# Hidden features of SwiGLU side by side, three tiles to an operation; first stage and last product rearranged

## The chip, the cores and the metric

The kernel runs on one core of one Trainium2 chip. The metric is the device time of one execution in microseconds (us). Engines are called as in the profile: PE is the matrix engine (PEld its weight loads), DVE the vector engine, ACT the activation engine, POOL the general one, SP the engine that does little but issue transfers. Each engine works through its own queue in order. On ACT and SP that queue also holds the transfers they issue, and a transfer whose data is not ready holds up what stands behind it.

## The reference

A gated recurrence with an outer product as state (4 batches, 8 heads, 768 tokens, head size 48), followed by a SwiGLU block on 3072 tokens of width 384 with 1536 inner features:

```python
f = 1.0 / (1.0 + np.exp(-f_logit))
for t in range(S):
    state = f[:, :, t, :, None] * state + np.einsum('bhd,bhe->bhde', k[:, :, t], v[:, :, t])
    y[:, :, t] = np.einsum('bhd,bhde->bhe', q[:, :, t], state)
x = y.transpose(0, 2, 1, 3).reshape(B * S, H * D)
g = x @ w_gate
out = (g * (1.0 / (1.0 + np.exp(-g))) * (x @ w_val)) @ w_out
```

The three weight arrays arrive in double precision and are turned into single precision on the chip. All else is float32.

## The kernel before

`short_path` does the work. A token chunk has 128 tokens of each of the four batches; there are six chunks, 0 to 5. The recurrence of one batch in one chunk is a *unit*; units 0 to 3 belong to chunk 0, units 4 to 7 to chunk 1, and so on. `attention(u)` (L518) is a generator that gives out one unit in 13 steps: gates (a sigmoid on ACT; for chunks 0 and 1 after PE has transposed f, for the later ones on f as it was loaded), a backward scan `tail` (L549), kT, a forward scan `head` (L562), qT, the scores `sc` (L586), their masking into A (L596), the product y, and the new state. `load` (L413) issues a unit's f, k, q and v transfers on SP.

**First stage** (up to L1157). Units 0 to 3 run one behind another (`run`). Between their steps the first weight pieces of 768 KB are fetched (`fetches`, SP), prepared by two ACT operations (`sizes`, L459 and L461) and put together by four or five DVE operations (`joins`, L467 to L473). The scratch of `sizes` has two buffers, so a `sizes` waits for the join two before it. The first four pairs of sizes and joins are half pieces: gate and val tile 0, gate and val tile 1. Then `mlp_plain(0)` begins: gate and val products of chunk 0 (L712) with Silu on ACT (L724) and a product on DVE (L728), together with the first steps of unit 4. `in_order` (L684) fixes the order of PE, DVE and ACT as written for this stage; SP's order is left to the planner.

**Second stage.** The rest of `mlp_plain(0)` takes turns with units 4 to 7. Here the planner decides the order of all engines. The down product of chunk 0 is `downs_abreast`.

**Third stage** (L1186 to L1219), chunks 1 to 5. The hidden products of a chunk are `mlp_fifteen` (L839). A product of 3x3 by 3x2 blocks is done with 15 instead of 18 block products. The token side has sums of token blocks, made by `token_sums` (L847) on DVE. One `triple(j)` covers the fifteen products (L887, four matmuls each: gate and val, two parts) of one of four sets of features. ACT copies a product's bank aside (L892), DVE adds and subtracts (L786, L789), and `finish` makes Silu (ACT, L903) and the product with val (DVE, L837). The triples come in the order 0, 2, 1, 3, so that hidden tiles with even numbers are complete after two of them. The down product is `down_seven` (L967), seven block products instead of eight. It needs sums of hidden blocks: `hidden_sums(j)` (two DVE operations per tile, for six tiles), then the first block of each tile is rewritten after `one` and the third after `two`. The seven are `one, six, two, three, four, five, seven`, each in two parts of 12 matmuls (L990; L1054 in `seven`), and `put_out` (L997) issues the result transfers.

A unit's steps, the token sums and the down weight sums enter by due times (`come_in`, L1191); the token sums of the next chunk are due two units of time before the chunk ends, thus ahead of the second part of `seven`. What is given to `lag` is written out one piece later, behind the next piece's matmuls. `in_order` fixes PE, DVE and ACT, not SP.

PSUM banks of this stage: tag A two, B one, o two (tag c shares them). A hidden tile is 128 partitions x 4 blocks x 256 tokens, six per chunk, a tag of six buffers (L702). `seven` writes both its halves into one bank of tag A. Its sums (`ob`) go out on ACT's queue, the last one of the kernel on SP's.

Of the kernel before, what the change touches and what calls it, by code (L numbers as in the profile page):

```python
# [9 lines left out]
FP32 = mybir.dt.float32  # L10
I32 = mybir.dt.int32
U32 = mybir.dt.uint32
AF = mybir.ActivationFunctionType
# [276 lines left out]
def short_path(ctx, tc, ident, least, judge, q, k, v, f_logit, moe_w_gate, moe_w_val, moe_w_out, out):  # L290
# [9 lines left out]
    nc = tc.nc  # L300
    B, H, S, D = q.shape
    C = 128
# [59 lines left out]
    def pairs(t, off=0):  # L362
        return t[:, off:off + HP * N1].rearrange("p (a t) -> p a t", t=N1)
# [151 lines left out]
    def bank(name):  # L515
        return banks[-1].tile([128, 512], FP32, tag="a", name=name)

    def attention(u):  # L518
        b, c = units[u]
        fr, kr, qr = (raw[nm][u % NRAW] for nm in "fkq")  # L520
# [10 lines left out]
        if c >= SQUARES:  # L531
            nc.scalar.activation(squares("f"), squares("f"), AF.Sigmoid)
        else:
            p = transposed("fTp", fr)
            nc.scalar.activation(pairs(gate)[:, :, 1:N1], p, AF.Sigmoid)
        yield
        if c >= SQUARES:
            nc.vector.transpose(in_turn(pairs(gate)[:, :, 1:N1]), squares("f"))
# [160 lines left out]
    TH = TB // 2  # L699
    FH = DFF // 2  # L700

    def hidden_tile():  # L702

        return ffn.tile([128, 4, TH], FP32, tag="h", name="h", bufs=NP)

    def mlp_plain(c):
        h = {}

        def product(w, j, name):
            p = fps.tile([128, 512], FP32, tag="m", name=name)[:, 0:TB]  # L710
            for i in range(KT):
                nc.tensor.matmul(p, lhsT=w[:, j, i, :], rhs=xT[c][:, i, :],  # L712
                                 start=(i == 0), stop=(i == KT - 1))
            return p

        def part(j):
            if j % NP not in h:
                h[j % NP] = hidden_tile()
            k = 2 * (j // NP)
            return h[j % NP][:, k:k + 2, :].rearrange("p a t -> p (a t)")  # L720

        def gate(j):
            p = product(w_gate, j, "gate")
            nc.scalar.activation(part(j), p, AF.Silu)  # L724

        def val(j):
            p = product(w_val, j, "val")
            nc.vector.tensor_tensor(part(j), part(j), p, ALU.mult)  # L728

        return ([lambda j=j, f=f: f(j) for f, j in ((gate, 0), (val, 0), (gate, 1), (val, 1))] +  # L730
                [lambda j=j, f=f: f(j) for i in range(2, NF, 2) for f in (gate, val) for j in (i, i + 1)],
                downs_abreast(c, h))

    def down_part(p, c, h, b, n):

        j = n // 2 + n % 2 * NP
        nc.tensor.matmul(p, lhsT=h[n // 2][:, n % 2 * 2 + b // 2, b % 2 * C:(b % 2 + 1) * C], rhs=w_out[:, j, :],  # L737
                         start=(n == 0), stop=(n == NF - 1))

    def out_rooms():  # L740
# [44 lines left out]
    def plus(dst, a, b):  # L785
        nc.vector.tensor_tensor(dst, a, b, ALU.add)  # L786
# [49 lines left out]
    def lag(f, *args):  # L836
        lagging.append(lambda: f(*args))  # L837

    def mlp_fifteen(c):  # L839
# [6 lines left out]

        def token_sums():  # L847
            x = comb.tile([128, 9, TH], FP32, tag="xs", name="xs")
            for n, nm in enumerate(("t14", "t15", "t8", "t9", "t2", "t1", "t4", "t11", "t5")):
                tokens[nm] = x[:, n, :]  # L850
            t = tokens
            minus(t["t14"], b21, b31)
            minus_both(t["t15"], b31, b32)
            plus(t["t8"], b21, t["t15"])
            plus(t["t9"], b12, b22)
            minus_both(t["t2"], t["t9"], t["t14"])
            plus(t["t1"], b12, b32)
            minus(t["t5"], b32, b11)
            plus(t["t4"], b11, t["t9"])
            minus_both(t["t11"], t["t4"], b21)  # L860
            plus(b12, b11, b12)
            plus(b31, b11, b31)
# [4 lines left out]

        def out_part(i, n, j):
            f = i * NJ + j
            if f % NP not in h:  # L870
                h[f % NP] = hidden_tile()
            return h[f % NP][:, 2 * (f // NP) + n, :]

        def triple(j):
            p, got = {}, {}
# [80 lines left out]
        order = list(range(0, NJ, 2)) + list(range(1, NJ, 2))  # L956
        pieces = [f for j in order for f in triple(j)]
        half = len(PRODUCTS) * (NJ // 2)
        ready = [sorted({(i * NJ + j) % NP for i in range(KT) for j in range(n, NJ, 2)}) for n in range(2)]
        for i, n in enumerate(ready[0]):  # L960
            pieces.insert(half + 10 + 3 * i, (0, lambda n=n: lag(hidden_sums, n)))
        pieces.append((0, finish_late))
        pieces.append(last[0])
        pieces += [(0, lambda n=n: lag(hidden_sums, n)) for n in ready[1]]
        return token_sums, pieces + last[1:]

    def down_seven(c, h):  # L967
# [1 line left out]


        DH = DM // 2
        s1 = [comb.tile([128, TH], FP32, tag=f"hs{j}", name=f"hs{j}") for j in range(NP)]
        b11, b12 = w_out[:, 0:NP, 0:DH], w_out[:, 0:NP, DH:DM]
        b21, b22 = w_out[:, NP:NF, 0:DH], w_out[:, NP:NF, DH:DM]
        kept = {}
        order = [*range(0, NP, 2), *range(1, NP, 2)]

        def hidden_sums(j):
            a11, a21, a12, a22 = (h[j][:, k, :] for k in range(4))
            plus(s1[j], a21, a22)  # L980
            minus(a21, a11, a21)

        def bank2(name, tag):
            pool = {"A": banks_a, "B": banks_b, "o": banks_o}[tag]
            return pool.tile([128, 512], FP32, tag=tag, name=name)[:, 0:DM].rearrange("p (n d) -> p n d", n=2)

        def add(p, lhsTs, rhs, first, part):
            for j in order[part * NP // 2:(part + 1) * NP // 2]:
                for n in range(2):
                    nc.tensor.matmul(p[:, n, :], lhsT=lhsTs[j][:, n * C:(n + 1) * C], rhs=rhs[:, j, :],  # L990
                                     start=first and j == order[0] and n == 0, stop=j == order[-1],
                                     skip_group_check=True)

        def of_h(k):
            return [h[j][:, k, :] for j in range(NP)]

        def put_out(half, n, queue):  # L997
            t0 = (2 * half + n) * S + c * C
# [2 lines left out]
        def one(part):  # L1001
            if part == 0:
                kept["o", 0], kept["o", 1] = out_rooms()
                kept["u"], kept["u5"] = (comb.tile([128, 2, TH], FP32, tag=t, name=t)[:, :, 0:DH]
                                         for t in ("c12", "c22"))
                kept["p"] = bank2("o11", "B")
            add(kept["p"], of_h(0), b11, True, part)
            if part:
                nc.scalar.copy(kept["u"], kept["p"])
                for j in order:  # L1010
                    lag(minus, h[j][:, 0, :], s1[j], h[j][:, 0, :])

        def two(part):
            add(kept["p"], of_h(2), b21, False, part)
            if part:
                nc.scalar.copy(kept["o", 0][:, :, 0:DH], kept["p"])
                for j in order:
                    lag(minus, h[j][:, 2, :], h[j][:, 2, :], h[j][:, 0, :])

        def three(part):  # L1020
            if part == 0:
# [5 lines left out]
        def four(part):  # L1027
            if part == 0:
                kept["p5"] = bank2("o5", "B")
            add(kept["p5"], s1, down_sums[1], True, part)  # L1030
            if part:
                lag(plus, kept["u5"], kept["u"], kept["p5"])

# [14 lines left out]
            add(kept["p4"], of_h(3), down_sums[4], True, part)  # L1048

        def seven(n):  # L1050
            if n == 0:
                kept["p"] = bank2("o3", "A")
            for j in order:
                nc.tensor.matmul(kept["p"][:, n, :], lhsT=h[j][:, 2, n * C:(n + 1) * C], rhs=b22[:, j, :],  # L1054
                                 start=n == 0 and j == order[0], stop=j == order[-1], skip_group_check=True)
            lag(plus, kept["o", 0][:, n, DH:DM], kept["u5"][:, n, :], kept["p"][:, n, :])
            lag(put_out, 0, n, nc.sync if n and c == NCH - 1 else nc.scalar)

        return hidden_sums, [(DOWN / 2, lambda f=f, part=part: f(part))
                             for f in (one, six, two, three, four, five, seven) for part in range(2)]  # L1060
# [45 lines left out]
    def run(b, *steps):  # L1106
        for s in steps:
            assert done[b] == s
            done[b] += 1
            for _ in range((3, 1, 4, 2, 3)[s]):  # L1110
                next(first[b])

    def load_ahead(u):

        if u + NRAW < B:
            load(u + NRAW, "fkq")
        load(u + 1, "v")
        fetches.pop(0)()
        if u + NRAW >= B:
            load(u + NRAW, "fkq")  # L1120

    run(0, 0, 1, 2)
# [1 line left out]
    for b in range(1, B):  # L1124
        if b == 1:
            run(1, 0)
            keep_warm(6)
        run(b, 1)
        run(b - 1, 3)
        run(b, 2)  # L1130
        load_ahead(b)
        if b + 1 < B:
            run(b + 1, 0)
        else:
            sizes.pop(0)()
        run(b - 1, 4)
    run(B - 1, 3)
    joins.pop(0)()
    run(B - 1, 4)

    hidden, last = mlp_plain(0)
    steps = attention_steps(1)
    for _ in range(2):
        sizes.pop(0)()
        joins.pop(0)()
    load(B + 1, "v")
    for _ in range(2):
        sizes.pop(0)()
    hidden[0]()
# [2 lines left out]
    joins.pop(0)()  # L1152
    hidden[1]()
    weights()
    hidden[2]()
    steps.pop(0)()
    in_order(mark, (mybir.EngineType.PE, mybir.EngineType.DVE, mybir.EngineType.Activation))  # L1157

# [135 lines left out]
```

## Time and profile before

| | us |
|---|---|
| median of 3 runs | 622.11 (620.12 to 622.82) |
| the profiled execution | 620.31 |
| its span | 618.6 |
| PE busy | 599.7 |
| DVE busy | 500.3 |
| ACT busy | 293.5 |
| first 52 us: PE busy / DVE busy | 43.75 / 44.00 |
| 147 to 210 us (fifteen products of chunk 1): PE / DVE | 62.54 / 60.73 |
| 244 to 307 us (the same of chunk 2): PE / DVE | 62.14 / 51.68 |

The profile comes from one execution. A line of a timeline reads: start, duration, engine, line of the kernel, operation, output and input, shape, and in brackets the idle time before it and what ended it. `x4` means four instructions drawn together. Matmuls overlap, so the duration of one line reaches into the next; the distance between starts is what one costs. A line of the waits reads: who waited, for whom, us in total, times, longest. PE's granted clock was full until the work ended (1.00 in every window to 584 us).

### The profile page before, as it was taken

Reading aid. Unit: us, or ns where it says so; the run is one execution under the profiler, and the core shown is the slowest. Engines: PE = TensorE matmul, PEld = TensorE weight load, DVE = VectorE, ACT = ScalarE, POOL = GpSimd, SP = SyncE. Lnnn points to the kernel's source line nnn. Section 1 sums busy time; section 2 is a strip of 40 time slices with the busy share of each in tenths; the row PEclk is TensorE's granted clock in tenths of the full one; section 3 lists DMA queues with packets and bytes.
Section 4 is the critical chain, followed back from the end, with each engine's and each line's share of the span. In section 5 each row is a group of like instructions: output and inputs, shape, how many; then the busy total and the mean of one; then the engine's idle time right before and its main releaser. Section 6 shows DMA issues by size and latency. Waiting matters only on the chain.

```text
span 618.6 us, 10913 instructions
## 1 busy us (share of the span) xinstructions
PE 599.7 (97%) x4060; PEld 490.1 (79%) x4060; DVE 500.3 (81%) x961; ACT 293.5 (47%) x535; POOL 5.0 (1%) x27
## 2 busy tenths in 40 slices
PE   7898999999999999999999999999999999999995
PEld 4744545667888898888899788899888889888895
DVE  7889999878999978868897877987887985566741
ACT  2485645313875621557711557632367640366600
POOL 1000000000000000000000000000000000000000
PEclk9999999999999999999999999999999999999998
DMA  9999583005231324222224320323321300100001
GB/s 150 236 246 254 172 231 92 5 23 161 63 86 51 85 61 125 69 48 64 51 77 117 91 52 19 84 62 95 107 75 33 81 6 10 52 2 0 1 2 56
DMA packets 95678, 50.95 MB, mean 82 GB/s; under 512 B 56064, under 2 KB 89472, under 8 KB 95616
## 3 DMA queue, kind: packets, MB, share of 16 engines
q1 hardware_dynamic: 92304, 45.64, 30.5%
q10 hardware_dynamic: 3312, 4.52, 2.0%
q8 instruction: 34, 0.56, 0.4%
q14 instruction: 28, 0.23, 0.1%
HBM read 42.47 MB, written 4.72 MB: 76 GB/s over the span
## 4 chain that ended last, share of the span: by engine, by line
PE 77%; DVE 12%; ACT 4%; DMA 3%; issue 2%; SPq 1%; ACTq 0%; DVEq 0%
PE o L990 16%; PE A L887 15%; PE B L887 11%; PE o L737 5%; PE o L887 5%; PE c L887 5%; PE sc L586 4%; PE val L712 4%; PE gate L712 3%; PE y L618 2%; PE kt L590 2%; PE y L614 1%; PE dS L659 1%; DVE head L562 1%; DMA fraw<-in_f_logit_dram 1%
## 5 line engine op out<-in xcount | busy, mean ns | idle before, releaser
L887 PE MATMUL A<-xs,w_both 128*128 128x256 f32 x240 | 62.6, 383 | 3.5 <-ACT c L892 2.3
L990 PE MATMUL o<-w_out,h 128*128 128x192 f32 x360 | 62.1, 328 | 0.2 <-ACT aside L892 0.2
L990 PEld LDWEIGHTS o<-w_out,h 128*128 128x128 f32 x360 | 58.6, 190 | 0.8 <-ACT aside L892 0.4
L887 PEld LDWEIGHTS A<-xs,w_both 128*128 128x128 f32 x240 | 44.5, 190 | 12.4 <-ACT c L892 3.9
L892 ACT COPY c<-A 128x512 f32<-128x512 f32 x40 | 23.3, 583 | 65.1 <-DVE ob L786 33.9
L786 DVE TENSOR_TENSOR c<-c,aside 128x512 f32<-128x512 f32 x60 | 41.1, 686 | 14.8 <-ACT aside L892 13.8
L892 ACT COPY aside<-A 128x512 f32<-128x512 f32 x60 | 35.0, 583 | 33.0 <-PE A L887 33.0
L789 DVE TENSOR_TENSOR c<-c,aside 128x512 f32<-128x512 f32 x60 | 41.2, 687 | 7.3 <-ACT aside L892 7.3
L837 DVE TENSOR_TENSOR h<-h,c 128x256 f32<-128x256 f32 x100 | 41.2, 421 | 7.0 <-ACT h L903 6.7
L990 PE MATMUL o<-ws,h 128*128 128x192 f32 x240 | 41.7, 328 | 0.0
L887 PE MATMUL B<-xT,extra 128*128 128x256 f32 x160 | 41.4, 382 | 0.0
L887 PE MATMUL c<-xT,w_both 128*128 128x256 f32 x160 | 41.3, 381 | 0.0
L887 PE MATMUL A<-xs,extra 128*128 128x256 f32 x160 | 41.2, 380 | 0.0
L887 PE MATMUL B<-xs,w_both 128*128 128x256 f32 x160 | 41.1, 380 | 0.0
L903 ACT ACTIVATE h<-c 128x256 f32<-128x256 f32 x100 | 39.2, 415 | 3.0 <-DVE c L789 1.9
L892 ACT COPY aside<-B 128x512 f32<-128x512 f32 x60 | 34.9, 582 | 10.6 <-PE B L887 10.2
L990 PEld LDWEIGHTS o<-ws,h 128*128 128x128 f32 x240 | 39.2, 190 | 0.3 <-issue 0.2
L789 DVE TENSOR_TENSOR c<-o,c 128x512 f32<-128x512 f32 x40 | 27.5, 689 | 14.6 <-ACT h L903 9.5
L596 DVE TENSOR_TENSOR A<-sc,causal 128x512 f32<-128x512 f32 x48 | 30.6, 678 | 6.0 <-PE sc L586 6.0
L887 PEld LDWEIGHTS B<-xs,w_both 128*128 128x128 f32 x160 | 30.4, 190 | 4.1
L887 PEld LDWEIGHTS c<-xT,w_both 128*128 128x128 f32 x160 | 30.2, 190 | 4.3 <-DVE c L789 0.2
L887 PEld LDWEIGHTS A<-xs,extra 128*128 128x128 f32 x160 | 30.3, 190 | 4.1
(134 smaller groups left out, 1155.0 us busy)
## 6 DMA issues: line engine op xcount, KB each, us to landing
fsquares<-in_f_logit_dram SPq DMA_DIRECT2D x64, 96.0 KB, 2.3
ksquares<-in_k_dram SPq DMA_DIRECT2D x64, 96.0 KB, 2.3
qsquares<-in_q_dram SPq DMA_DIRECT2D x64, 96.0 KB, 2.3
v<-in_v_dram SPq DMA_DIRECT2D x24, 192.0 KB, 3.3
w<-in_moe_w_gate_dram SPq DMA_DIRECT2D x6, 768.0 KB, 6.1
w<-in_moe_w_val_dram SPq DMA_DIRECT2D x6, 768.0 KB, 5.6
w<-in_moe_w_out_dram SPq DMA_DIRECT2D x6, 768.0 KB, 5.3
out_dram<-ob ACTq DMA_DIRECT2D x23, 192.0 KB, 2.0
```

The lines of the kernel that those rows point to most:

```text
L586: nc.tensor.matmul(sc[par][:, a * C:(a + 1) * C], lhsT=kT[r, a, :], rhs=qT[r, a, :], start=True, stop=True)
L590: nc.tensor.transpose(p[:, a * C:(a + 1) * C], kT[:, a, :], ident)
L596: nc.vector.tensor_tensor(A[:, par], sc[par].rearrange("p (a t) -> p a t", t=C), causal.unsqueeze(1).broadcast_to((128, HP, C)), ALU.mult)
L712: nc.tensor.matmul(p, lhsT=w[:, j, i, :], rhs=xT[c][:, i, :], start=(i == 0), stop=(i == KT - 1))
L737: nc.tensor.matmul(p, lhsT=h[n // 2][:, n % 2 * 2 + b // 2, b % 2 * C:(b % 2 + 1) * C], rhs=w_out[:, j, :], start=(n == 0), stop=(n == NF ...
L786: nc.vector.tensor_tensor(dst, a, b, ALU.add)
L789: nc.vector.tensor_tensor(dst, a, b, ALU.subtract)
L837: lagging.append(lambda: f(*args))
L887: nc.tensor.matmul(p[name][:, n, :], lhsT=weights_of[a][:, n, j, :], rhs=tokens[b], start=fresh and n == 0, stop=True, skip_group_check=True)
L892: nc.scalar.copy(t, p[name])
L903: nc.scalar.activation(dst, src[:, 0, :], AF.Silu)
L990: nc.tensor.matmul(p[:, n, :], lhsT=lhsTs[j][:, n * C:(n + 1) * C], rhs=rhs[:, j, :], start=first and j == order[0] and n == 0, stop=j == ...
```

## The change

1. **Hidden tiles.** Two tiles of 128 x 3 x 4 x 256 instead of six of 128 x 4 x 256: one holds features 0, 2, 4, the other 1, 3, 5. `hidden_sums` and the two rewritings handle three features in one operation. The even sums are all due after the twelfth product of the third triple, where they were due after products 10, 12 and 14.
2. **Token sums.** t9 and t1, which stand beside each other now, are made in one operation of 2 x 256.
3. **seven.** Each half has a bank of its own, the first of tag A, the second of tag o; all its result transfers go out on SP.
4. **First stage.** Unit 4's sigmoid is taken on f as loaded, before the first Silu; behind the transposition stands a Copy. The first three sizes and joins move up by a step. Unit 5's f, k and q are loaded together with its v, later. SP's order is fixed as written too.

```diff
+    ahead = set()
+    def sigmoid_ahead(u):
+        fr = raw["f"][u % NRAW]
+        nc.scalar.activation(fr, fr, AF.Sigmoid)
+        ahead.add(u)
@@ attention
-            nc.scalar.activation(pairs(gate)[:, :, 1:N1], p, AF.Sigmoid)
+            nc.scalar.activation(pairs(gate)[:, :, 1:N1], p, AF.Copy if u in ahead else AF.Sigmoid)
@@ hidden tiles
-    def hidden_tile():
-        return ffn.tile([128, 4, TH], FP32, tag="h", name="h", bufs=NP)
+    def hidden_tile(h, j):
+        if j % 2 not in h:
+            h[j % 2] = ffn.tile([128, NP // 2, 4, TH], FP32, tag="h", name="h", bufs=2)
+        return h[j % 2][:, j // 2]
@@ token_sums
-            for n, nm in enumerate(("t14", "t15", "t8", "t9", "t2", "t1", "t4", "t11", "t5")):
+            for n, nm in enumerate(("t14", "t15", "t8", "t9", "t1", "t2", "t4", "t11", "t5")):
...
-            plus(t["t9"], b12, b22)
+            two = (128, 2, TH)
+            plus(x[:, 3:5], b12.unsqueeze(1).broadcast_to(two), xT[c][:, 1:3, TH:2 * TH])
             minus_both(t["t2"], t["t9"], t["t14"])
-            plus(t["t1"], b12, b32)
@@ mlp_fifteen, order of the pieces
-        for i, n in enumerate(ready[0]):
-            pieces.insert(half + 10 + 3 * i, (0, lambda n=n: lag(hidden_sums, n)))
-        pieces.append((0, finish_late))
-        pieces.append(last[0])
-        pieces += [(0, lambda n=n: lag(hidden_sums, n)) for n in ready[1]]
+        pieces.insert(half + 12, (0, lambda: lag(hidden_sums, 0)))
+        pieces += [(0, finish_late), last[0], (0, lambda: lag(hidden_sums, 1))]
@@ down_seven
-        def hidden_sums(j):
-            a11, a21, a12, a22 = (h[j][:, k, :] for k in range(4))
-            plus(s1[j], a21, a22)
+        def hidden_sums(odd):
+            a11, a21, a12, a22 = (h[odd][:, :, k, :] for k in range(4))
+            plus(s1[odd], a21, a22)
             minus(a21, a11, a21)
...
-                for j in order:
-                    lag(minus, h[j][:, 0, :], s1[j], h[j][:, 0, :])
+                for odd in range(2):
+                    lag(minus, h[odd][:, :, 0, :], s1[odd], h[odd][:, :, 0, :])
...
-                for j in order:
-                    lag(minus, h[j][:, 2, :], h[j][:, 2, :], h[j][:, 0, :])
+                for odd in range(2):
+                    lag(minus, h[odd][:, :, 2, :], h[odd][:, :, 2, :], h[odd][:, :, 0, :])
...
         def seven(n):
-            if n == 0:
-                kept["p"] = bank2("o3", "A")
+            p = bank2("o3", "Ao"[n])[:, n, :]
             for j in order:
...
-            lag(put_out, 0, n, nc.sync if n and c == NCH - 1 else nc.scalar)
+            lag(put_out, 0, n, nc.sync)
@@ first stage
-        if u + NRAW >= B:
+        if u + NRAW == B:
             load(u + NRAW, "fkq")
...
+    joins.pop(0)()
+    sizes.pop(0)()
     run(B - 1, 3)
+    sizes.pop(0)()
     joins.pop(0)()
     run(B - 1, 4)
...
-    for _ in range(2):
-        sizes.pop(0)()
-        joins.pop(0)()
-    load(B + 1, "v")
+    sigmoid_ahead(B)
+    joins.pop(0)()
     for _ in range(2):
         sizes.pop(0)()
     hidden[0]()
...
     weights()
+    load(B + 1)
     hidden[2]()
     steps.pop(0)()
-    in_order(mark, (mybir.EngineType.PE, mybir.EngineType.DVE, mybir.EngineType.Activation))
+    in_order(mark, (mybir.EngineType.PE, mybir.EngineType.DVE, mybir.EngineType.Activation, mybir.EngineType.SP))
```

## The prediction

> **What bounds the kernel now.** First the page's busy line: PE is busy 599.7 of 618.6 us. So the time is PE's work plus PE's gaps, and what another engine gives up counts only where it ends a gap.
>
> ```profile
> span 618.6 us, 10913 instructions
> PE 599.7 (97%) x4060; PEld 490.1 (79%) x4060; DVE 500.3 (81%) x961; ACT 293.5 (47%) x535; POOL 5.0 (1%) x27
> ```
>
> Second, the waits of PE: who ended a gap, total us, times, longest.
>
> ```profile
> PE sc L586 <- DVE qT L568: 3.3, 3, 1.8
> PE A L887 <- ACT c L892: 2.3, 4, 0.6
> PE A L887 <- ACT aside L892: 1.3, 5, 0.3
> ```
>
> DVE, 81% busy, ends no gap after the first 52 us. ACT, 47% busy, ends nine of them. Third, the timeline of ACT and of PE at the beginning of a block of fifteen products (chunk 1 ends, chunk 2 begins; the other three look alike).
>
> ```profile
> 241.66 4.71 ACTq L999 DMA_DIRECT2D out_dram<-ob  x3
> 246.41 0.58 ACT L892 COPY c<-A 128x512 f32<-128x512 f32 x1 [8.62 <-DVE ob L786]
> ```
>
> ```profile
> 245.45 1.03 PE L887 MATMUL o<-xT,w_both 128*128 128x256 f32 x4
> 247.05 1.13 PE L887 MATMUL A<-xs,w_both 128*128 128x256 f32 x4 [0.57 <-ACT c L892]
> 248.02 1.03 PE L887 MATMUL B<-xT,extra 128*128 128x256 f32 x4
> ```
>
> ACT holds the result transfers of the last quarter of the output. They wait for DVE's last sums (ob), which DVE makes after the token sums, at 245.6 to 246.2. Behind them in ACT's queue stands the copy of product 0, which was ready near 244.8. PE's product 3 needs a bank of tag A and stalls. Last, the end of the first stage and of the kernel.
>
> ```profile
> 39.28 1.28 ACT L535 ACT_TABLE_LOAD   x1
> 42.78 0.56 DVE L467 TENSOR_SCALAR top<-top 128x768 f32<-128x768 f32 x1 [1.59 <-ACT top L461]
> 46.38 1.22 DVE L549 TENSOR_TENSOR_SCAN tails<-gates,ones 128x516 f32<-128x516 f32 x1
> 51.67 1.16 PE L586 MATMUL sc<-qT,kT 48*128 48x128 f32 x16 [1.81 <-DVE qT L568]
> ```
>
> ```profile
> 611.98 0.62 DVE L786 TENSOR_TENSOR ob<-c,o 128x192 f32<-128x192 f32 x2 [2.29 <-PE o L1054]
> 612.66 0.38 SPq L999 DMA_DIRECT2D out_dram<-ob  x1
> ```
>
> **Result transfers from ACT to SP (seven).** Two issues of some 0.35 us leave ACT per chunk, and so does their wait. The copy of product 0 then starts at 244.8 and ends at 245.4; product 3 is due at 245.45 + 0.865 (the spacing of products) = 246.31. If it takes the bank of the first last product instead, that is free when DVE has read it, near 245.9: also in time. What a stall costs is read from product 4: due at 247.18, it began at 248.02, so 0.84 (0.57 of gap, the rest refilling). Four boundaries: 3.4 us. Against this speaks the Trainium skill, "DMA: Bandwidth & Descriptors", section "Issuing engines are not separate DMA queues": all issuing engines feed the same 16 DMA engines, and another issuer saves only the issue time, usually small. By that rule ACT gains 0.7 us a chunk and PE nothing. The row decides otherwise: what ACT loses is not the issue but 8.62 us of waiting in front of a copy, which the rule doesn't speak of. I take 3.4; by the rule it is 0, and that end goes into the range. On SP the two wait until 246.2; the next transfers behind them are the f loads at 252.23, which the transposed gates release at 251. Nothing is held up.
>
> **Separate banks for the last product.** The second half takes a bank of tag o. Its two slots held six's and five's sums, which DVE has read by 241.63 and 240.5; PE wants one at 241.77. Cost 0, at most 0.3 a chunk (one short gap), 1.5 in all. Inside a chunk DVE makes the token sums first, so the early read pays only at the very end: there the first half's sum need no longer wait for 611.98 but starts at 610.0, the second's at 611.98 instead of 612.25, and its transfer is issued 0.3 earlier. That transfer took 3.9 us to land while its neighbour flew beside it; a pair at 609.7 took 2.6 and 2.8, pairs at the chunk boundaries 1.9. Alone I take 2.8: 0.3 + 1.1 = 1.4, between 0.3 and 2.3.
>
> **The beginning.** Unit 4's sigmoid moves in front of the Silus and its later activation is a Copy: the table loads at 39.28 and 42.76 go (1.28 each), one activation of 128x512 (0.60) comes. Two size pairs (1.1 each) and a join (1.9) move up by one step. DVE idles 1.25 before the masking of unit 3 at 27.86: the first join fills it and pushes the masking to 28.5, and that unit's last copy, which the first gate product needs, ends near 31.0. The first gate product now starts at 31.14 waiting for that join: no change. Followed forward on ACT and DVE in their order (a size pair may start when the join two before it has ended): joins end at 31.6, 33.4, 35.3 and 38.3; Silu's remaining load at 35.2, Silu to 37.0, the Copy to 37.6, sizes of the fourth weight piece (landed at 36.3) to 39.3, its join to 42.4. Behind that join DVE has unit 4's scan: 42.4 instead of 46.38. From scan to sc is 5.3 us, so sc is ready at 47.7, before PE asks at 49.9: the 1.81 go. The Trainium skill, "ScalarE: Activation LUTs", section "What ACT_TABLE_LOAD costs", puts a switch at 2.66 us, a 1.38 drain included. The trace has 1.29 from the load at 37.37 to its Silu at 38.66, so no drain is paid here. By the page the remaining load would put the scan at 43.8 and sc at 49.1: still in time, so the sum is the same by both. Between 39 and 50 PE's order is the planner's, not written out; if it keeps sc too early the gain is nothing. I take 1.8, ends 0 and 2.
>
> SP's order is now fixed here. Its sequence of bytes is nearly the present one: unit 3's f lands behind the same weight piece (19.3). Unit 5's f, k, q move behind the fifth piece and land near 44 instead of 38 to 41; PE uses f at 59.27, a cover of 15 us. Unit 6's k and q wait on SP for unit 4's transposes (39.4 to 40.4) and hold up the sixth piece, fetched at 40.64 today: under 1 us, PE needs it at 62. Without these covers each would cost what it is late.
>
> **Three tiles side by side.** Per chunk 24 operations of 128x256 become 8 of 128x768. Six in a row take 2.10, so one costs 0.34. A strided 128x1152 took 1.35 and 128x512 takes 0.69, 1.03 ns an element; so 768 take 0.95, or 0.86 in a row.
>
> ```profile
> 201.27 1.35 DVE L789 TENSOR_TENSOR ws<-w_out,ws 128x1152 f32<-128x1152 f32 x1
> 219.54 2.10 DVE L789 TENSOR_TENSOR h<-hs,h 128x256 f32<-128x256 f32 x6
> ```
>
> 24 x 0.335 = 8.0 against 8 x 0.86 = 6.9; the joined token sum saves another 0.08. DVE gains 1.2 a chunk, 6 in all, and on the path 0: no gap of PE in these stages names DVE. The even sums now come as one block of 1.7 at the twelfth product instead of 0.7 thrice; what follows it on DVE (sums that free asides) is up to 1.05 later, once a chunk. ACT's asides wait for that, and PE for ACT. I take 0, since three asides and two A banks lie between; all of it passed on would be 5.3. The two h tiles become free with the last product of a chunk; their first new write is the Silu at product 9, 10 us later.
>
> **Sum.** 618.6 - 3.4 - 1.4 - 1.8 = 612.0 span. The profiled run took 620.31 (1.7 around the span) and lies 1.8 below the median of the runs shown, 622.11. So 613.7 in such a run, 615.5 against the median.
>
> **Rivals.**
> 1. The transfers help, the rest doesn't (planner keeps sc early, the last transfer lands in 3.9): 622.1 - 3.4 - 0.3 = 618.4. For it: PE's order there is unknown. Against: DVE's chain has 4 us taken out.
> 2. The blocks of merged sums reach PE: + 5.3 on 615.5, 620.8. For it: from 147 to 210 DVE is busy 60.7 of 63, and ACT waits there for DVE's h. Against: in the later chunks it is busy 51.7 of 63, and less work is left in total.
> 3. Slower: a merged operation walks all three features of one plane with holes between; if waits were set by its whole stretch, a plane written would hold up PE's reading of the other planes. At the chunk's end six's odd half would wait 0.4 for the odd sums, two 1.5 for the rewritten first plane, three's second half 1.7 for the third: 3.6 plus three refills of 0.27, 4.4 a chunk, 22 in all: 637. It decides from 2 us a chunk on. Against it: the first f load (columns 0 to 47 of 64) went out at 0.80 while the program's earlier fill of columns 48 to 63 ran at 1.65, so interleaved regions are told apart.
>
> ```profile
> 0.80 0.46 SPq L430 DMA_DIRECT2D fraw<-in_f_logit_dram  x1
> 1.65 0.34 POOL L341 MEMSET fraw<- 128x128 f32 x2
> ```
>
> **How the numbers follow.** My forecast 0.56, its own range 613 to 618; rival 1 0.15; rival 2 0.17; rival 3, or some wait like it, 0.12. About 0.5% (3.1 us) is what a measurement of this kernel can tell from no change. Forecast and rival 1 are faster: 0.71, less a little for 618.4 lying near the bound of 619.0: 0.70. Rival 2 is the same, 0.17, slower 0.13. The range 612.5 to 622 leaves out rival 3 and the edges.
>
> **What will show it.** Right: no gap of PE at L887 behind ACT's c copies at the four boundaries; ACT's copy of product 0 within 0.2 of its product; out transfers on SP; one pair of table loads fewer before 50 us and no gap before unit 4's sc; 8 operations of 128x768 of about 0.95 a chunk; the last two sums 2 us apart. Wrong: a new gap in front of the second last product (bank o), PE gaps at products 0 to 3 of the triple behind the merged sums, or DVE waiting for PE inside the down stage.

## The result and the profile after

The changed kernel takes 616.81 us (median of 4 runs, 616.57 to 617.18). The kernel before, run beside it, took 621.22. The ratio is 0.9927, with a 95% interval from 0.9901 to 0.9954. The profiled execution took 616.57, and its span is 614.8 where it was 618.6: 3.8 us less. The runs of the kernel before fall into two groups, 620.1 to 621.3 at a mean granted clock of 0.996 or more and 621.7 to 622.9 at 0.993 or 0.994, and as its four runs here are two of each, the 3.8 between the profiled spans is a better measure than the 4.4 between the medians.

The busy lines of the page after:

```profile
span 614.8 us, 10801 instructions
PE 598.2 (97%) x4060; PEld 489.8 (80%) x4060; DVE 493.5 (80%) x876; ACT 291.5 (47%) x534; POOL 5.0 (1%) x27
```

PE is still busy for all but 16.6 us. DVE gave up 6.8 us and ACT 2.0, but that alone says nothing about the time. The waits of PE in the kernel after (who waited for whom, total, times, longest) say more:

```profile
PE fTp L536 <- DMA fraw<-in_f_logit_dram: 2.4, 2, 1.9
PE sc L595 <- DVE qT L577: 1.5, 2, 0.8
PE A L895 <- ACT aside L900: 1.3, 5, 0.3
PE y L648 <- ACT kt L603: 0.7, 1, 0.7
PE o L747 <- DVE h L738: 0.7, 1, 0.7
PE qTp L536 <- DMA qraw<-in_q_dram: 0.6, 1, 0.6
PE sc L595 <- ACT state L673: 0.5, 1, 0.5
```

The four waits for ACT's c copies (2.3) are gone and so is the wait of 1.8 for qT. Five entries are new or larger: f from memory (2.4, 1.9 at one time; it was 1.7, at most 0.8), kt, o behind DVE's h, q from memory and the state. All five lie in the part up to chunk 1.

At the beginning of a block of fifteen (chunk 2), ACT, PE and SP now look like this:

```profile
244.87 0.59 ACT L900 COPY c<-A 128x512 f32<-128x512 f32 x1 [7.00 <-DMA out_dram<-ob]
246.32 0.59 ACT L900 COPY c<-B 128x512 f32<-128x512 f32 x1 [0.87 <-DVE ob L796]
```

```profile
243.80 1.03 PE L895 MATMUL A<-xs,w_both 128*128 128x256 f32 x4
245.53 1.03 PE L895 MATMUL o<-xT,w_both 128*128 128x256 f32 x4
246.39 1.02 PE L895 MATMUL A<-xs,w_both 128*128 128x256 f32 x4
247.26 1.03 PE L895 MATMUL B<-xT,extra 128*128 128x256 f32 x4
```

```profile
246.00 0.85 SPq L1003 DMA_DIRECT2D out_dram<-ob  x2
```

ACT copies product 0 at 244.87 instead of 246.41. Product 0 runs from 243.80 to 244.83, so the copy follows it at once: what ended ACT's 7.00 of idling is the product, although the bracket names a transfer. ACT's next copy waits for DVE (0.87), but PE has a bank by then, and its products follow each other every 0.865. The two transfers wait on SP, where nothing is held up: the next transfer there is issued at 251.47.

The first stage and its end, first on PE:

```profile
20.37 0.63 PE L536 MATMUL fTp<-idf,fraw 128*128 128x128 f32 x4 [1.92 <-DMA fraw<-in_f_logit_dram]
31.93 2.84 PE L724 MATMUL gate<-xT,w_both 128*128 128x512 f32 x6
49.09 1.16 PE L595 MATMUL sc<-qT,kT 48*128 48x128 f32 x16
105.87 2.10 PE L747 MATMUL o<-w_out,h 128*128 128x384 f32 x6
108.67 0.91 PE L747 MATMUL o<-w_out,h 128*128 128x384 f32 x2 [0.70 <-DVE h L738]
```

Then the one table load that is left there on ACT, and DVE at unit 4's scan and ahead of the gap at 108:

```profile
36.16 1.28 ACT L734 ACT_TABLE_LOAD   x1
```

```profile
43.66 1.23 DVE L558 TENSOR_TENSOR_SCAN tails<-gates,ones 128x516 f32<-128x516 f32 x1
...
104.68 0.56 DVE L469 TENSOR_SCALAR top<-top 128x768 int32<-128x768 int32 x1
105.27 0.96 DVE L471 SCALAR_TENSOR_TENSOR top<-w,top 128x768 int32<-128x768 int32 x1
106.15 0.68 DVE L738 TENSOR_TENSOR h<-h,val 128x512 f32<-128x512 f32 x1
106.74 0.69 DVE L568 TENSOR_TENSOR kT<-kTp,tails 128x512 f32<-128x512 f32 x1
107.34 0.68 DVE L577 TENSOR_TENSOR qT<-qTp,head 128x512 f32<-128x512 f32 x1
107.94 0.68 DVE L738 TENSOR_TENSOR h<-h,val 128x512 f32<-128x512 f32 x1
```

Unit 4's sc runs at 49.09 without a gap, where it waited until 51.67. The down product begins at 105.87, 0.88 earlier than before (106.75). Then PE stops at 107.97 for 0.70. It wants the bank that the last val product fills, and DVE reads that bank in its last multiplication, from 107.94 to 108.62. Before the change DVE did this from 107.78 to 108.46, and PE came just late enough not to notice. So the first product of chunk 1 comes at 147.42; before it was 147.33. The new beginning has brought nothing.

The kernel's end, DVE and SP:

```profile
606.69 0.35 DVE L796 TENSOR_TENSOR ob<-c,o 128x192 f32<-128x192 f32 x1 [0.34 <-PE o L1057]
608.64 0.35 DVE L796 TENSOR_TENSOR ob<-c,o 128x192 f32<-128x192 f32 x1 [1.60 <-PE o L1057]
```

```profile
607.10 2.25 SPq L1003 DMA_DIRECT2D out_dram<-ob  x2
```

The last two sums are 1.95 apart, as each half has its bank. The very last transfer lands at most 3.6 after its issue (it was 3.9).

The merged operations, in the groups of DVE by shape:

```profile
L799 DVE TENSOR_TENSOR h<-h 128x768 f32<-128x768 f32 x20 | 19.0, 953 | 5.7 <-PE o L994 5.1
L796 DVE TENSOR_TENSOR hs<-h 128x768 f32<-128x768 f32 x10 | 9.5, 954 | 0.0
L799 DVE TENSOR_TENSOR h<-hs,h 128x768 f32<-128x768 f32 x10 | 9.1, 948 | 0.0
```

Eight a chunk, 0.95 each. No gap of PE names them.

The whole can be read from three marks in each trace: when the first product of chunk 1 starts, when the last product of the kernel (`seven` of chunk 5) starts, and the span. They split the time into the part up to chunk 1, the five chunks with their products of fifteen and of seven ("fifteens"), and the tail.

| | to chunk 1 | fifteens | tail | span |
|---|---|---|---|---|
| before | 147.33 | 460.54 | 10.7 | 618.6 |
| after | 147.42 | 457.11 | 10.3 | 614.8 |
| difference | +0.1 | −3.4 | −0.5 | −3.8 |

### The profile page after: what moved, and what is told of

It is laid out like the page before. It is cut to its first block, busy times and chain, and to the rows that moved or that the text cites. A ratio compares the mean times of both kernels' runs of the same rounds, so it can differ in the third digit from the quotient of the medians.

```text
span 614.8 us, 10801 instructions
## 1 busy us (share of the span) xinstructions
PE 598.2 (97%) x4060; PEld 489.8 (80%) x4060; DVE 493.5 (80%) x876; ACT 291.5 (47%) x534; POOL 5.0 (1%) x27
## 4 chain that ended last, share of the span: by engine, by line
PE 91%; DVE 4%; ACT 2%; DMA 1%; issue 1%; ACTq 0%; DVEq 0%
PE o L994 19%; PE A L895 16%; PE B L895 13%; PE o L895 5%; PE gate L724 5%; PE val L724 5%; PE o L747 5%; PE c L895 5%; PE sc L595 4%; PE o L1057 3%; PE y L627 2%; PE y L648 2%; PE kt L599 2%; PE dS L668 1%; PE y L623 1%; DMA fraw<-in_f_logit_dram 1%
## 5 line engine op out<-in xcount | busy, mean ns | idle before, releaser
L900 ACT COPY aside<-B 128x512 f32<-128x512 f32 x60 | 35.0, 584 | 10.1 <-PE B L895 10.1
```

The costliest lines, as they stand in the source:

```text
L900: nc.scalar.copy(t, p[name])
```

## The experiments

The same split for all runs comes first, so that each run can be found in it. Ratios are against the kernel before on the same chip.

| run | to chunk 1 | fifteens | tail | span | median | ratio (95%) |
|---|---|---|---|---|---|---|
| SP transfers only | 147.40 | 457.20 | 10.8 | 615.4 | 617.64 | 0.9955 (0.9941–0.9969) |
| first stage only | 147.44 | 460.45 | 10.8 | 618.7 | 620.77 | 0.9999 (0.9988–1.0011) |
| merging only | 147.79 | 460.18 | 10.5 | 618.5 | 621.11 | 1.0004 (0.9993–1.0016) |
| banks only | 147.31 | 460.56 | 10.1 | 618.0 | 620.20 | 0.9996 (0.9984–1.0007) |
| after, SP not ordered | 151.65 | 457.09 | 10.5 | 619.2 | 620.91 | 0.9980 (0.9963–0.9997) |
| after, weight sums later | 147.37 | 457.09 | 10.1 | 614.6 | 616.04 | 0.9902 (0.9885–0.9918) |
| both of these | 151.86 | 456.77 | 10.5 | 619.1 | 620.88 | 0.9971 (0.9955–0.9986) |
| after, last transfer in two | 147.68 | 457.09 | 10.8 | 615.6 | 617.77 | 0.9931 (0.9914–0.9947) |
| after, old first stage | 147.32 | 457.09 | 10.1 | 614.5 | 616.60 | 0.9930 (0.9916–0.9945) |
| after, no clamp | 148.40 | 457.08 | 10.1 | 615.6 | 617.46 | 0.9945 (0.9927–0.9963) |
| after, no clamp, old first stage | 146.90 | 457.09 | 10.1 | 614.1 | 615.88 | 0.9916 (0.9901–0.9931) |
| after, joins later | 151.26 | 457.66 | 10.4 | 619.3 | 620.28 | 0.9984 (0.9973–0.9994) |

**The transfers alone.** The kernel before with one line changed:

```diff
-            lag(put_out, 0, n, nc.sync if n and c == NCH - 1 else nc.scalar)
+            lag(put_out, 0, n, nc.sync)
```

> The kernel before with one line changed: all of seven's result transfers go out on SP. My theory (ACT's queue was held by the transfers' wait): the four gaps of PE behind ACT's copies of product 0 vanish, 0.84 each, span shorter by 3.3 to 3.5, so nearly all of what the whole change brought (3.8 in span). Rival (only the issue time of 0.35 leaves ACT): the four gaps stay, time unchanged within 0.5. End of the kernel as before.

The boundary to chunk 2 in this kernel:

```profile
244.85 0.59 ACT L892 COPY c<-A 128x512 f32<-128x512 f32 x1 [7.00 <-DMA out_dram<-ob]
246.05 0.85 SPq L999 DMA_DIRECT2D out_dram<-ob  x2
```

The copy starts 1.56 earlier than before the change (246.41), which is more than the 0.7 of two issues: the waiting transfer held it up. The span fell by 3.2, and the five chunks by 3.3. The c copies are gone from the waits of PE. This line is nearly the whole change.

**The first stage alone.** The kernel before with `sigmoid_ahead`, the new sequence of sizes, joins and loads, and SP's order fixed:

```diff
+    joins.pop(0)()
+    sizes.pop(0)()
     run(B - 1, 3)
+    sizes.pop(0)()
...
+    sigmoid_ahead(B)
...
+    in_order(mark, (mybir.EngineType.PE, mybir.EngineType.DVE, mybir.EngineType.Activation, mybir.EngineType.SP))
```

> The kernel before with the new first stage alone. Theory from the profile after (the gain of the beginning is given back at the start of the down product of chunk 0, where PE waits for DVE's last product with val): unit 4's sc near 49 instead of 51.7, a gap of 0.5 to 0.9 near 108 behind DVE, and the first product of chunk 1 at 147.3 to 147.6; time unchanged within 0.5. Rival (the beginning does bring its 0.9 and the gap near 108 comes from another part of the change): first product of chunk 1 near 146.4, span shorter by 0.9.

Nothing was gained. PE in this kernel:

```profile
108.70 0.91 PE L746 MATMUL o<-w_out,h 128*128 128x384 f32 x2 [0.67 <-DVE h L737]
```

The gap at 108 is there with none of the other parts, so it belongs to the new first stage.

**The merging alone.** The kernel before with the two wide hidden tiles, the merged sums and the joined token sum.

```diff
-            plus(s1[j], a21, a22)
+            plus(s1[odd], a21, a22)
```

> The kernel before with the two wide hidden tiles, the merged sums and the joined token sum alone. Theory: DVE is busy some 6 to 7 us less, the four gaps stay, span unchanged within 0.3. Rival 2 (blocks of merged sums reach PE): longer by 1 to 5, with gaps of PE in products 0 to 3 of the last triple.

DVE's busy time fell from 500.3 to 492.7. The four gaps stayed:

```profile
PE A L895 <- ACT c L900: 2.0, 4, 0.5
```

The time didn't move. Some 7.6 us of DVE work were taken off and were worth, in the chunks, the 0.36 that the split shows; 0.3 of that is in the four gaps, which shrank from 2.3 to 2.0. In the span it doesn't show, as chunk 1 began 0.46 late in this execution: already the first sc, which the edit doesn't touch, came at 11.32 instead of 10.31.

**The banks alone.** The kernel before with one bank for each half of `seven`, transfers left on ACT.

```diff
-            if n == 0:
-                kept["p"] = bank2("o3", "A")
+            p = bank2("o3", "Ao"[n])[:, n, :]
```

> The kernel before with a bank of its own for each half of seven alone; transfers stay on ACT. Theory: at the kernel's end the first half's sum starts 2.0 earlier, the last one 0.27 earlier; the last transfer lands 3.6 to 3.9 after its issue whether alone or not, span shorter by 0.3 to 0.5; at the chunk boundaries the four gaps stay. Rival (the neighbour slowed the last transfer): span shorter by 1.4. Loss possible: a short gap at seven's second half behind bank o, up to 0.3 a chunk.

The tail is 0.6 shorter and the rest unchanged. In the nine traces with these banks and one last transfer the tail is 10.1 to 10.5, in the four without them 10.5 to 10.8, so about 0.5 is the banks' part. The spans of the four parts add up: −3.2 + 0.1 − 0.1 − 0.6 = −3.8, the difference between before and after. That it fits to the tenth is luck. In the chunks the transfers alone bring 3.34 and the merging alone 0.36, and the whole change 3.43: what the merging gains there it takes from the same four gaps.

**SP's order left to the planner.** Why does the new first stage fix it?

```diff
-    in_order(mark, (mybir.EngineType.PE, mybir.EngineType.DVE, mybir.EngineType.Activation, mybir.EngineType.SP))
+    in_order(mark, (mybir.EngineType.PE, mybir.EngineType.DVE, mybir.EngineType.Activation))
```

> The changed kernel, but SP's order in the first stage is again left to the planner. In the changed kernel the sixth weight piece went out at 45.8 instead of 40.6 and DVE stood idle 1.3 for it at 53. Theory S (that delay is what made DVE late at the start of the down product): the sixth piece goes out near 41, the gap of PE near 108 behind DVE vanishes, first product of chunk 1 at 146.4 to 146.7, span 613.9. Theory D (DVE's queue up to 108 is full whatever the weights do): the gap near 108 stays between 0.4 and 1, first product at 147.3 to 147.6, span 614.8 within 0.4.

Neither theory had this. DVE and PE in this kernel:

```profile
44.63 0.56 DVE L467 TENSOR_SCALAR top<-top 128x768 f32<-128x768 f32 x1 [3.01 <-ACT top L461]
```

```profile
51.40 2.08 PE L595 MATMUL sc<-qT,kT 48*128 48x128 f32 x16 [3.32 <-DVE qT L577]
```

The planner fetched the fifth weight piece at 37.23; with SP ordered it is fetched at 33.80. A join of that piece stands in front of unit 4's scan on DVE and waited 3.0. So the new sequence on DVE needs the load order that came with it. But the wait is only a part of the 4.2 by which chunk 1 began later. The same products behind unit 4's sc, here and in the profile after:

```profile
54.32 6.87 PE L724 MATMUL val<-xT,w_both 128*128 128x512 f32 x12
```

```profile
50.67 5.32 PE L724 MATMUL val<-xT,w_both 128*128 128x512 f32 x12
```

From PE's gap on the granted clock was lower: 0.83 from 48 to 52, 0.50 from 52 to 56 and 0.82 from 56 to 60. From the start of that sc to the next gate products it took 9.62 instead of 6.73. Thus sc came 2.3 later, 2.9 were lost to the clock, and 1.0 was won back, as there is no gap at 108. The ten runs differ accordingly: one, with a mean granted clock of 0.998, took 617.79, two with 0.995 took 619.1 and 619.5, and seven with 0.993 took 620.5 to 621.7.

The written order may have a price of its own: unit 3's f reaches PE at 20.37 instead of 19.49 in this run, and the first gate product starts at 31.93 instead of 31.05. The 0.88 is handed on in full. The transfer is issued at the same time in both and lands 7.0 instead of 6.0 later. Of the six traces with the written order five have 6.8 to 7.5; the one of the next run has 6.1, so the order alone doesn't decide it.

**Weight sums later.** What frees DVE before 108? Three groups of weight sums for the next stage were put behind the gate and val products:

```diff
-    for n, at in enumerate((5, 6, 8)):
-        hidden.insert(hidden.index(weights, 3 * at), lambda n=n: behind(lambda: [t[n]() for t in sums_of]))
-    take_turns(hidden + weave(last, sums_of[0][3:7] + sums_of[1][3:7] + sums_of[0][7:] + sums_of[1][7:]), steps, 8)
+    take_turns(hidden + weave(last, sums_of[0][0:7] + sums_of[1][0:7] + sums_of[0][7:] + sums_of[1][7:]), steps, 8)
```

> The changed kernel with the first three pairs of token-independent weight sums (six operations, 3.9 of DVE) moved from between the gate and val products to behind the down product's beginning. Theory D (DVE's work before 108 sets when the last product with val frees its bank): the gap near 108 vanishes, first product of chunk 1 some 0.9 earlier, at 146.5, span 613.9. Theory S (the late weight piece alone): DVE still late by the weights, gap stays at 0.7. If DVE is then late in the down stage or at the token sums, a new gap shows behind 108, and the gain is smaller.

The gap at 108 went (down product from 106.52 without a break), but unit 4's sc waited 1.12 at 49.73 and another one 0.40 at 130.40. Chunk 1 began at 147.37. The wait at 49.73 is not the edit's doing: it lies in the first stage, which is the same here as in the changed kernel. There ACT waited for the fifth weight piece:

```profile
41.21 0.92 ACT L459 ACTIVATE up<-w 128x768 int32<-128x768 uint32 x1 [1.43 <-DMA w<-in_moe_w_gate_dram]
```

In the profile after that wait was 0.28. DVE's last multiplication ended at 107.24, 1.4 earlier than in the changed kernel, so it would have been in time for PE there as well (107.97). What stands ahead of it in DVE's queue made the gap at 108; whether taking it away brings the 0.9 to chunk 1 stays open. The four runs have spans of 613.7, 614.0, 614.6 (the profiled one) and 615.2, and two of them are what was expected of it; the changed kernel's are 614.8 to 615.4.

**Both of these.** SP left to the planner and the sums later:

> The two edits of the runs before at once. Theory D: like the moved sums alone, span 613.9. Theory S: like the free SP order alone. If each carries a part, shorter than either, down to 613.4.

The sc of unit 4 waited 4.46 at 52.61, chunk 1 began at 151.86. The granted clock fell behind the gap here too, to 0.60 from 52 to 56. So this run is as late as the one with the free order alone, from a longer wait and a shorter time at a low clock, and it says nothing on the later sums.

**The last transfer in two halves** of 64 rows, one on SP and one on ACT, issued at 609.25 and 609.31:

```diff
+        def put_halves(n):
+            t0 = n * S + c * C
+            for r, queue in ((0, nc.sync), (64, nc.scalar)):
+                queue.dma_start(out=out[t0 + r:t0 + r + 64, :], in_=kept["o", 0][r:r + 64, n, :])
```

> The changed kernel with its very last result transfer cut in two halves of 64 rows, one issued on SP and one on ACT. In the changed kernel the last transfer took 3.6 to land, its bulk had moved 1.7 after the issue, the rest trickled. If the time goes by the amount that each transfer carries, it lands 0.5 to 1 sooner and the span is shorter by as much; if something else at the end of the program holds a few packets, landing stays at 3.4 to 3.9 and the span within 0.3.

The halves landed 3.0 and up to 3.4 after their issue, the single transfer 3.6: halving the amount took at most 0.6 off. The tail was 10.8 all the same, where it is 10.1 to 10.5 with one transfer. What passed between the landing and the end of the span grew from 2.2 to 2.9; why is not known. In this run the granted clock was 0.97 from 16 to 31 us and 0.85 from 31 to 40, and the first gate product came at 33.13, 1.2 later than in the profile after. Yet chunk 1 began only 0.26 later: the gap at 108 wasn't there. Most of the lateness went into the slack in front of DVE's last multiplication.

**The old first stage in the changed kernel.**

```diff
-    sigmoid_ahead(B)
-    joins.pop(0)()
+    for _ in range(2):
+        sizes.pop(0)()
+        joins.pop(0)()
+    load(B + 1, "v")
...
```

> The changed kernel with the first stage of the kernel before (order, loads, table loads and SP left to the planner there). Theory: the new first stage is worth nothing by the start of chunk 1, so the first product of chunk 1 comes at 147.3 to 147.5, unit 4's sc has its gap of 1.8 again, there is no gap in front of the last part of the down product at 108, and the span is 614.8 as in the changed kernel. Rival: what the parts gave alone does not add up, and the new beginning is worth its 1.8 beside the other parts: span 616.6. Against the kernel before: ratio 0.993 by the theory, 0.996 by the rival.

By the theory, to 0.3 us: the changed kernel without its new beginning is just as fast.

**Without the clamp.** The clamp of the weights at L467 is left out of the join (20 operations, 10.3 us of DVE before 120); weights outside single precision's range would come out wrong. It was run with the new and with the old first stage.

```diff
-            nc.vector.tensor_scalar(top.bitcast(FP32), top.bitcast(FP32), as_float(0x38000000), as_float(0x47F00000),
-                                    op0=ALU.max, op1=ALU.min)
```

> The changed kernel without the clamp of the weights' exponents at L467 (20 operations of DVE, 10 us by the trace, all before 120 us; weights beyond single precision's range would come out wrong, the rest of the joining is done). Theory: up to 147 the engine that sets the time is DVE; its products with val hold the bank that the down product needs at 108, and its joins hold the masking of unit 3 and with it the first gate product. With 10 us less before 120 the gap at 108 goes (0.9) and the first gate product comes up to 0.5 earlier: first product of chunk 1 at 146.0 to 146.6, span 613.4 to 614.0. Rival: what PE has lost before 147 is set by arrival of the loads and by PE's own work; then DVE idles more, the first product of chunk 1 stays at 147.4 and the span at 614.8.

> The same clamp left out, with the first stage of the kernel before. Theory: three clamps stand ahead of unit 4's scan behind 38 us, so the gap of 1.8 before its sc shrinks by about 1 to 1.7; nothing is given back at 108, so the first product of chunk 1 comes at 146.2 to 146.8. The new first stage is then worth 0 to 0.5 with DVE relieved too (difference to the run without the clamp that has the new first stage). Rival: the new first stage shows its worth once DVE no longer takes it back: this run at 147.4, the other at 146 or before, 1.4 apart.

With the old first stage it went as the theory said in kind, less in size: unit 4's sc still waited 1.35 (1.78 with the clamp; it was to shrink by 1 or more), and chunk 1 began at 146.90, 0.4 earlier (expected 0.5 to 1.1). DVE's last multiplication now waits for PE, not PE for it:

```profile
106.21 0.69 DVE L736 TENSOR_TENSOR h<-h,val 128x512 f32<-128x512 f32 x1 [1.57 <-PE val L722]
```

With the new first stage both expectations missed the beginning of chunk 1. The first gate product did come earlier, at 31.47 instead of 31.93, as the theory had it. DVE has 9.6 us less to do from 31 to 147, and chunk 1 begins 1.0 *later*. The gap at 108 is gone, but there is another one. DVE and PE in this kernel:

```profile
79.75 0.56 DVE L467 TENSOR_SCALAR top<-top 128x768 int32<-128x768 int32 x1 [1.80 <-ACT top L461]
80.23 0.68 DVE L566 TENSOR_TENSOR kT<-kTp,tails 128x512 f32<-128x512 f32 x1
80.83 0.68 DVE L575 TENSOR_TENSOR qT<-qTp,head 128x512 f32<-128x512 f32 x1
```

```profile
81.65 1.16 PE L593 MATMUL sc<-qT,kT 48*128 48x128 f32 x16 [1.66 <-DVE qT L575]
```

The planner has put a join of a later weight in front of kT and qT. ACT prepares that weight only from 78.03, DVE stands still for 1.80, and PE's sc behind it for 1.66. So here the time of the second stage followed from what stood in front of kT, qT and the multiplications in DVE's queue, and not from the total of DVE's work.

**Joins later.** If joins of down weights hold the multiplication at 108, move two of them to the down product, and tie DVE's later work behind the last multiplication:

```diff
+    for _ in range(2):
+        del hidden[max(i for i, f in enumerate(hidden) if f is weights)]
     for i in range(len(joins) - hidden.count(weights)):
         last.insert(3 * i, weights)
...
+    on_dve = [[ins for ins in part if ins.engine == mybir.EngineType.DVE] for part in (traced[:begun[0]], traced[begun[0]:])]
+    keep_order([on_dve[0][-1], on_dve[1][0]])
+    for ins in on_dve[1][1:]:
+        keep_order([on_dve[0][-1], ins])
```

> The changed kernel with two of the weight preparations of the second stage moved from between the last gate and val products to the down product, and with DVE's later work tied behind the last val multiplication (L738). Nothing is left out. Theory: the 0.9 that the new first stage brought as far as the down product was given back because DVE worked at joins of down weights, which are not needed before 120, ahead of the multiplication that frees PE's bank; with two joins fewer in front that multiplication comes by 106.5, the gap at 108.7 goes, the first product of chunk 1 comes at 146.4 to 146.7 and the span is 613.8 to 614.1. Rival: the order of the second stage that comes out of it puts the wait in front of another score product or down product; then the first product of chunk 1 stays at 147.3 or later, and the span at 614.7 or more.

The gap at 108 went here too, and the run was no better than the kernel before the change. PE's waits in it from 106 to 152:

```profile
PE o L747 <- DVE w_out L473: 1.8, 3, 1.1
```

`weights` also fetches and prepares. Moving it put off the last fetch of a down weight from 92.92 to 103.1, and the down product caught up with the joins. From the start of the down product to chunk 1 this kernel takes 43.5; the kernel before took 40.6. PE's three waits are 1.8 of these 2.9. The clock was 0.89 from 16 to 31 us in this trace and the first gate product at 33.88, which also made it late by 2.0 at the start, in a part that the edit doesn't touch. The profiled execution took 621.05, the median is 620.28 and the best of twelve runs 618.83, so the edit loses in the others too. No run of the study beat the changed kernel by more than the intervals: the two lowest medians, 616.04 and 615.88, are 0.1% and 0.2% below it, with ratios whose intervals overlap its own.

## Why the prediction was right, and where not

The forecast was 615.5, and 616.81 was measured, inside its own range of 613 to 618. Worked in spans it was 612.0 against 614.8: of its three terms (3.4, 1.4 and 1.8) the first came, the second brought 0.5 and the third nothing. By its own steps:

**Result transfers to SP: right, in mechanism and in size.** Predicted 3.4, measured 3.3 by the one line alone (460.54 to 457.20 in the fifteens) and 3.4 in the whole. The four gaps are gone, product 4 of chunk 2 moved from 248.02 to 247.26, and nothing on SP is held up. The Trainium skill's rule in "DMA: Bandwidth & Descriptors", section "Issuing engines are not separate DMA queues", would have given 0. It speaks of the transfers' speed and of the time to issue them; that a copy stands behind a waiting transfer lies outside it, and this decided. One reading was wrong without harm to the sum: the 8.62 is all of ACT's idling in front of the copy, and 7.00 of it are there after the change too, when there is nothing to copy yet. What the transfer cost ACT is 1.5 (246.41 against 244.87). And only the first of the two stood ahead of the copy: the second was issued at 246.49.

**The banks and the end: the first half right, the second wrong.** No gap came in front of the second half (cost put at 0 to 0.3 a chunk). The step "its transfer is issued 0.3 earlier" holds: the last transfer is issued 4.5 after the start of the last product instead of 4.8. "Alone I take 2.8" failed: it landed in up to 3.6, nearly the 3.9 of before. Altogether 0.5 to 0.6 instead of 1.4. The neighbour in flight made 0.3 of the last transfer's length at most, and half the amount still took 3.0 to 3.4. What sets it, while pairs in the middle of the run land in 1.9, stays open.

**The beginning: wrong, 0 instead of 1.8.** Within it most steps came true: two loads fewer, the scan at 43.66 (predicted 42.4), sc without a gap. The one load left runs from 36.16, and its Silu begins at 37.45: 1.29, so here as before no drain shows, though the scan came near the 43.8 that the 2.66 of the Trainium skill's "ScalarE: Activation LUTs" (section "What ACT_TABLE_LOAD costs") would have made. Three steps failed.

- "Its sequence of bytes is nearly the present one: unit 3's f lands behind the same weight piece (19.3)." PE had it at 20.37. With SP's order free it was 19.49, and the first gate product shifted by the same 0.88. The transfer took 7.0 where it had taken 6.0; why stays open, as one trace with the same order has 6.1.
- "Under 1 us" for the sixth weight piece: it was fetched at 45.78 instead of 40.64, behind unit 5's f, k, q and v, all of which the written order puts in front of it. DVE idled 1.29 for that piece at 53.15. PE shows no gap from it.
- The sum stopped at sc. Taking a gap away at 51 makes PE earlier at all that follows, and the question was who meets it next. In the kernel before, DVE had been busy 54.0 of 56.6 us from 52 to 108.6, and its last multiplication freed PE's bank only at 108.46. The gain arrived there as 0.88, and the next sc came at 109.52 where it had come at 109.42: all of it was lost in the gap and its refilling. The first stage alone (0.9999) and the old first stage in the new kernel (614.5) show that this is all of it.

**Merged sums: right.** 0.95 each as estimated, no effect on the path, no wait between planes. DVE's busy time fell by 7.6 with the merging alone, and 6 had been worked out for it. Beside the moved transfers at most 0.1 of it reached the path (457.20 to 457.11 in the chunks).

**Rivals.** The third, waits between planes, fell: no gap of PE names a hidden tile. So did the second: alone, the merged sums gave 1.0004. The first, "the transfers help, the rest doesn't", describes what happened better than the forecast: its 3.4 + 0.3 is 3.7 of the 3.8 measured in spans. Its 618.4 was counted from 622.11; from the 621.22 that the kernel before took beside the new one it would be 617.5. The medians differ by 0.7 more than the spans, because the profiled execution of before lies 0.9 below its median and that of after 0.2. That 616.81 lies in the range is thus luck in part: the range was wide enough to hold a forecast of which only the first term came true.

## What to carry to other kernels

Here a transfer that waited for its data held up what stood behind it in the queue of the engine that issued it. In another kernel, look in the timeline for a long wait of a DMA issue on an engine with other work, and read the price from the distance of the starts of what comes after on the bound engine (here 0.84 at each of four boundaries). When a stall is taken away, follow the gain on to the next place where the bound engine needs something from a full engine; here DVE was busy for 54.0 of 56.6 us, and the 0.9 ended there. Where a planner orders the queues, less work on an engine can cost time, because another order comes out and puts an operation that waits in front of one that is needed, as in the run without the clamp. And before a lost time is put down to an edit, look at the granted clock and at what was already late ahead of the edited part: here several runs can't be read without both.

## What was not expected of the hardware

- The last transfer of the program took 3.6 to land alone and 3.9 in company, where the result transfers of the profile after take 1.9 at the least and 2.2 in the median. In two halves on two queues it took up to 3.4, and the tail was longer.
- With the new first stage and SP's order fixed, PE idles for 1.7 to 2.5 us in front of unit 3's f in five of six traces. In two of them the granted clock fell: to 0.58 from 20 to 24, directly behind a gap of 2.5 (first gate product 2.0 later), and to 0.77 and 0.80 from 28 to 36, some 8 us behind a gap of 2.0 (1.2 later). In the other three it stayed at 1.00, and so it did behind the gap of 1.8 at 51.67 before the change. No trace with the old first stage shows a fall. With SP left to the planner the gaps were 3.3 and 4.5, and the clock fell to 0.50 and 0.60 from 52 to 56. Whether the gaps cause it wasn't tried.
